# Attention softmax in a fused kernel: epsilon and reciprocal on 128x9 sums ahead of the turn, a copy behind it, and a new written order

## Chip, cores, metric

The kernel runs on one core of a Trainium2 chip. The metric is the device time in microseconds; the time given is the median of several runs, and beside it stands one execution that the hardware profiler recorded.

## What is computed

Causal attention over B = 4, H = 8, S = 576, D = 64 feeds a gated MLP (`moe`), and this feeds a channel mix (`moe2`). The part that the change touches is the division of the softmax:

```python
def _attn_ref(q, k, v, s):
    ...
    scores = np.where(causal, -1000000000.0, scores + np.minimum(bias, 0.0))
    scores = scores - np.max(scores, axis=-1, keepdims=True)
    attn = np.exp(scores)
    attn = attn / (np.sum(attn, axis=-1, keepdims=True) + 1e-09)
    return np.matmul(attn, v).astype(np.float32)
...
def reference(**kwargs):
    ...
    attn_out = _attn_ref(**attn_kwargs)
    ...
    x = _moe_ref(x=x, **moe_kwargs)
    return _moe2_ref(x=x, **moe2_kwargs)
```

All data are 32-bit floats. Products are split into a rounded high part and a remainder, so one product is several matmuls (`ka`/`qa` and `KB`/`QB` for the scores, `wsg0`/`wsg1`, `gh`/`gl` and so on).

## The kernel before

**Attention.** `attn_pair` handles two heads at a time: 16 pairs, numbered 0 to 15, four for each batch. A pair takes nine steps over row tiles of 128: four of the first head (`st<pair>_0_0` to `_0_3`), one with the last 64 rows of both heads (`_2_4`), four of the second head (`_1_0` to `_1_3`). In a step TensorE writes scores into a PSUM bank (`sc`, three banks); VectorE adds the mask, writes the scores to `st` and their row minimum to `mx` (the custom operation, ISA in the order, which is followed by a read of its accumulator into `mx`); ScalarE takes the exponential in place and adds its row sums into one column of `sums0` or `sums1` (128x9, even and odd pairs); TensorE turns the tile (`tp`, and for the last rows `tq`), and ScalarE or VectorE copies it to `pt1` or `pt2` for the product with the values (`pv`, then `xT`). The names in the profile leave the numbers out: `st` is any of the tiles `st5_1_3` and so on.

**End of a pair.** TensorE turns the raw sums (`rt`, 9x128, in PSUM), VectorE adds the epsilon (`rc<-rt`) and takes the reciprocal in place (`rc<-rc`). SyncE stores `rc` in DRAM (`rdram`) and loads it three times, spread over the partitions (`rb`). Later VectorE multiplies `xT` by `rb` (`scale_pending`).

**The rest.** Once a batch has its four pairs, `moe1` runs for it between the pairs of the next batches: `v` and `u` are matmuls whose results go through a gelu on ScalarE and VectorE (steps `v0_2`, `u0_3`: batch 0, tile 2 or 3), `v` is normalised (BN_STATS, BN_AGGR, then `vn`), `sg` mixes along the sequence, and VectorE writes `ga` from it. VectorE also prepares weights in the gaps: `wcs`, `wsg`, `wy`, `syt` are steps of the split of weights, and SyncE stores `wcs` in DRAM (`wscr`). The channel mix with its large products (`k`, `r`) fills the time behind the attention.

**The order.** Each engine runs its instructions in one written order. `ORDER` holds for each engine a list of instruction numbers (numbers in the order in which the code issues them to that engine); `Lines.written` turns the list into the order of the program. An instruction issued with `extra` has no number and stands just ahead of the next numbered one. An engine therefore waits at its next instruction even where a later one could run. Nearly every instruction goes through one helper and so shows as L193 in the profile of before (L194 after the change); the tiles tell them apart.

Of the kernel before, what the change touches and what calls it, by code (L numbers as in the profile page):

```python
# [8 lines left out]
F32 = mybir.dt.float32  # L9
# [3 lines left out]
ALU = mybir.AluOpType  # L13
# [4 lines left out]
P = 128  # L18
# [10 lines left out]
SUM_EPS = 1e-9  # L29
# [51 lines left out]
    ),  # L81
    "vector": (
# [140 lines left out]
def fused_kernel(ctx, tc, kqT, vL, s, w_in, g_ln, w_sgT, b_sg, w_out, mu_k, mu_r, w_k, w_v, w_r, out):  # L223
    nc = Lines(tc.nc)
# [899 lines left out]
```

## Time and profile before

| | before |
|---|---|
| median of 3 runs | 648.51 us (647.1 to 648.82) |
| profiled execution, its own time | 650.21 us |
| profiled execution, span | 648.3 us, mean granted TensorE clock 0.992 |
| TensorE matmul (PE) busy | 619.1 us, 96% of the span |
| TensorE weight load (PEld) busy | 538.1 us, 83% |
| VectorE (DVE) busy | 470.7 us, 73% |
| ScalarE (ACT) busy | 414.7 us, 64% |
| GpSimd (POOL) busy | 244.9 us, 38% |
| chain that ended last | PE 80%, DVE 7%, DMA 6%, ACT 3% |

The span runs from the first to the last instruction of the execution; its own time has 1.9 us more outside it. Busy shares are means over all stages of the kernel; what binds in one stage is read from that stage. A number in brackets in a row of a timeline is the time that the engine sat idle before the row, and behind the arrow stands what ended it. SPq rows are DMAs being issued by SyncE. Successive operations of one engine overlap by a little in the rows, so the distance between two starts is what one costs the queue.

### The profile page before, as it was taken

How to read it: one execution, taken by the hardware profiler on the slowest of the kernel's cores; microseconds unless marked ns; L12 is line 12 of the kernel's file. 1: busy time of each engine (PE TensorE's matmuls, PEld its weight loads, DVE VectorE, ACT ScalarE, POOL GpSimd, SP SyncE). 2: the span in 40 equal slices, each digit the busy share in tenths (PEclk: the TensorE clock that was granted, in tenths of full speed). 3: DMA queues.
4: the chain of work that ended last, by engine and by line, in shares of the span. 5: the costliest groups of instructions: out<-in, count | busy, mean ns of one | idle time of the engine just before them, and what ended most of it. 6: DMA issues, size and time to landing. Idle time of an engine off the chain costs nothing.

```text
span 648.3 us, 11385 instructions
## 1 busy us (share of the span) xinstructions
PE 619.1 (96%) x3768; PEld 538.1 (83%) x3768; DVE 470.7 (73%) x986; ACT 414.7 (64%) x937; POOL 244.9 (38%) x319
## 2 busy tenths in 40 slices
PE   1789999989999999999999999999999999999997
PEld 1667777878778997888897999888888888999997
DVE  6889679995659744569632978478897869696964
ACT  4889889974648834669631864268776778553530
POOL 7466769999629687279371200000000000000000
PEclk9789999999999999999999999999999999999999
DMA  7776574464653643734314974576665794646543
GB/s 216 186 238 198 156 212 110 151 211 114 187 194 94 178 132 81 244 93 135 112 23 146 316 260 125 145 243 199 238 213 196 223 342 151 200 160 206 206 146 122
DMA packets 68522, 115.09 MB, mean 178 GB/s; under 512 B 19744, under 2 KB 32688, under 8 KB 68464
## 3 DMA queue, kind: packets, MB, share of 16 engines
q1 hardware_dynamic: 68464, 114.37, 56.6%
q8 instruction: 30, 0.49, 0.3%
q14 instruction: 28, 0.23, 0.1%
HBM read 75.63 MB, written 29.20 MB: 162 GB/s over the span
## 4 chain that ended last, share of the span: by engine, by line
PE 80%; DVE 7%; DMA 6%; ACT 3%; issue 1%; SPq 1%; POOL 1%; DVEq 0%; ACTq 0%
PE k L193 15%; PE sg L193 8%; PE psa L193 8%; PE r L193 8%; PE o L193 6%; PE sc L193 6%; PE v L193 6%; PE u L193 6%; PE pv L193 6%; PE tp L193 4%; PE psb L193 4%; PE psc L193 2%; DMA wsr<-in_w_sgT_dram 1%; DVE st L193 1%; DMA sraw<-in_w_in_dram 1%
## 5 line engine op out<-in xcount | busy, mean ns | idle before, releaser
L193 PE MATMUL k<-x,wk 128*128 128x512 f32 (+1 forms) x480 | 98.9, 368 | 0.0
L193 PEld LDWEIGHTS k<-x,wk 128*128 128x128 f32 x480 | 83.6, 189 | 14.9
L193 ACT ACTIVATE st<-st,mx 128x384 f32<-128x384 f32 (+4 forms) x128 | 75.1, 588 | 20.2 <-DVE mx L193 18.7
L193 PE MATMUL sc<-ka,qa 128*128 128x512 f32 (+3 forms) x180 | 61.5, 358 | 19.4 <-DMA ka<-ka 13.3
L193 DVE CUSTOM_DVE_ANT_0 st<-sc,mask 128x512 f32<-128x512 f32 (+3 forms) x128 | 62.4, 502 | 13.5 <-PE sc L193 12.5
L193 PE MATMUL sg<-wsg,vn 128*128 128x288 f32 x448 | 63.6, 297 | 0.8 <-DVE ga L193 0.8
L193 PEld LDWEIGHTS sg<-wsg,vn 128*128 128x128 f32 x448 | 60.4, 188 | 1.7 <-DVE ga L193 1.0
L193 PE MATMUL tp<-ident,st 128*128 128x128 f32 x344 | 56.2, 281 | 4.0 <-ACT st L193 3.5
L193 PE MATMUL sc<-KB,QB 128*128 128x512 f32 (+3 forms) x180 | 57.1, 337 | 0.0
L193 PEld LDWEIGHTS sc<-ka,qa 128*128 128x128 f32 x180 | 33.4, 188 | 26.6 <-ACT ka L193 12.5
L193 PEld LDWEIGHTS tp<-ident,st 128*128 128x128 f32 x344 | 42.5, 144 | 10.6 <-ACT st L193 4.2
L193 PE MATMUL pv<-pt,vf 128*64 128x320 f32 (+4 forms) x448 | 51.3, 364 | 0.0
L193 ACT COPY pt<-tp 128x384 f32<-128x384 f32 (+1 forms) x88 | 43.5, 508 | 9.8 <-PE tp L193 9.6
L193 PE MATMUL r<-x,wr 128*128 128x512 f32 (+1 forms) x240 | 49.5, 368 | 0.0
L193 PE MATMUL v<-wv,xs 128*128 128x512 f32 x192 | 48.7, 398 | 0.0
L193 ACT ACTIVATE yx<-yt,mu 128x64 f32<-128x64 f32 (+4 forms) x64 | 30.4, 529 | 27.9 <-DMA yt<-ydram 27.9
L193 PEld LDWEIGHTS r<-x,wr 128*128 128x128 f32 x240 | 41.9, 189 | 7.5
L193 PEld LDWEIGHTS pv<-pt,vf 128*64 128x64 f32 x448 | 29.6, 136 | 20.8 <-issue 3.3
L193 DVE SCALAR_TENSOR_TENSOR yx<-yt,mu,yx 128x64 f32<-128x64 f32 (+4 forms) x64 | 31.1, 514 | 14.6 <-ACT yx L193 14.4
L193 PE MATMUL u<-xs,wc 128*128 128x288 f32 x288 | 41.3, 297 | 0.0
L193 PEld LDWEIGHTS v<-wv,xs 128*128 128x128 f32 x192 | 35.0, 188 | 7.0
L193 PEld LDWEIGHTS u<-xs,wc 128*128 128x128 f32 x288 | 39.2, 188 | 0.5
(184 smaller groups left out, 1420.9 us busy)
## 6 DMA issues: line engine op xcount, KB each, us to landing
wc<-wscr SPq DMA_DIRECT2D x24, 512.0 KB
kq<-in_kqT_dram SPq DMA_DIRECT2D x32, 288.0 KB
kr<-kdram SPq DMA_DIRECT2D x12, 768.0 KB
kdram<-k SPq DMA_DIRECT2D x16, 512.0 KB
yt<-ydram SPq DMA_DIRECT2D x24, 257.0 KB
vf<-in_vL_dram SPq DMA_DIRECT2D x16, 320.0 KB
gt<-gdram SPq DMA_DIRECT2D x12, 384.0 KB
out_dram<-t SPq DMA_DIRECT2D x24, 192.0 KB
```

The source lines that it names most:

```text
L193: r = f(*a, **k)
```

## The change

The epsilon is added and the reciprocal taken on the sums as they lie, 128x9 in SBUF, before TensorE turns them. TensorE then turns the reciprocals, and VectorE copies the turned 9x128 from PSUM to `rc`. The add is an `extra` instruction, so the numbers of all others are kept: the number of the old add is now the reciprocal's, the number of the old reciprocal the copy's. Four of the five lists of `ORDER` are written anew (tensor, vector, scalar, gpsimd; sync is unchanged); of these one line is shown.

```diff
 ORDER = {
...
-        "461 439 443-444 474-475 460 462 465 450 458 466 452 451 476 456 463 467-468 464 469-470 472 471 473 "
+        "461 439 443-444 474-475 460 462 465 450 466 458 452 451 476 456 463 467-468 464 469-470 472 471 473 "
...
+    seps = const.tile([P, 1], F32, tag="seps", name="seps")
...
+    nc.vector.extra(lambda: nc.nc.vector.memset(seps, SUM_EPS))
     nc.gpsimd.memset(mhalf, -0.5)
...
             yield (i + 1) * 200
+        nc.vector.extra(lambda: nc.nc.vector.scalar_tensor_tensor(out=sm, in0=sm, scalar=1.0, in1=seps.broadcast_to([P, 9]), op0=ALU.mult, op1=ALU.add))
+        nc.vector.reciprocal(sm, sm)
         rt = psum1.tile([P, 512], F32, tag="acc", name=f"rt{pr}", bufs=3)
         nc.tensor.transpose(rt[:9, :P], sm, ident)
         rc = at.tile([9, P], F32, tag="rc", name=f"rc{pr}", bufs=1)
-        nc.vector.tensor_scalar_add(rc, rt[:9, :P], SUM_EPS)
-        nc.vector.reciprocal(rc, rc)
+        nc.vector.tensor_copy(rc, rt[:9, :P])
         nc.sync.dma_start(out=rdram[pr], in_=rc)
```

On TensorE `rt` keeps its place among its neighbours, but for pairs 3 and 5, where one matmul or a few change sides. On VectorE three places are shown, before and after; in all of them the last number of a name is a running number of the program and differs between the two.

The first place is VectorE about 41 us into the execution, where pair 1 ends and pair 2 begins. `tq1` is the turned last tile of pair 1, `xT0<-xT0,rb0` the late scaling of pair 0, `wcs0` a weight step. Before:

```order
L193 TENSOR_TENSOR xT0_147<-xT0_147,rb0_309 128x576
L193 ISA st1_1_3_463,mx1_1_3_464<-sc1_1_3_0_465,mask_88 128x512
L193 ISA mx1_1_3_464 128x1
L193 ISA st_f2_555,mx2_0_0_556<-sc2_0_0_0_557,mask_88 128x128
L193 ISA mx2_0_0_556 128x1
L193 COPY pt2_1_366<-tq1_428 128x2x64
L193 TENSOR_TENSOR wcs0_478<-syt4_477,wcs0_478 128x512
L193 ISA st_f2_555,mx2_0_1_562<-sc2_0_1_0_563,mask_88 128x256
```

The same place after the change:

```order
L194 COPY pt2_1_369<-tq1_431 128x2x64
L194 TENSOR_TENSOR xT0_149<-xT0_149,rb0_312 128x576
L194 ISA st1_1_3_466,mx1_1_3_467<-sc1_1_3_0_468,mask_89 128x512
L194 ISA mx1_1_3_467 128x1
L194 TENSOR_TENSOR wcs0_481<-syt4_480,wcs0_481 128x512
L194 ISA st_f2_559,mx2_0_0_560<-sc2_0_0_0_561,mask_89 128x128
L194 ISA mx2_0_0_560 128x1
L194 ISA st_f2_559,mx2_0_1_566<-sc2_0_1_0_567,mask_89 128x256
```

The copy out of `tq1` has moved from behind `st1_1_3` and the first tile of pair 2 to ahead of the scaling of `xT0`, and `wcs0` one step forward.

The second place is VectorE about 98 us into the execution, at the end of pair 5, among the steps of `v` of batch 0. Before:

```order
L193 SCALAR_TENSOR_TENSOR v0_1028<-v0_1028,v0_2_1128 128x512
L193 ISA st5_1_3_1345,mx5_1_3_1346<-sc5_1_3_0_1347,mask_88 128x512
L193 ISA mx5_1_3_1346 128x1
L193 TENSOR_TENSOR wsg1_101<-wsr4_1316,wsg0_100 128x576
L193 SCALAR_TENSOR_TENSOR v0_1028<-v0_1028,v0_2_1128 128x512
L193 COPY pt2_5_1186<-tq5_1281 128x2x64
L193 BN_STATS st6_0_1029<-v0_1028 128x6
L193 ISA st6_0_0_1509,mx6_0_0_1510<-sc6_0_0_0_1511,mask_88 128x128
L193 ISA mx6_0_0_1510 128x1
L193 ISA st6_0_1_1516,mx6_0_1_1517<-sc6_0_1_0_1518,mask_88 128x256
```

And after:

```order
L194 SCALAR_TENSOR_TENSOR v0_1034<-v0_1034,v0_2_1135 128x512
L194 COPY pt2_5_1193<-tq5_1288 128x2x64
L194 ISA st5_1_3_1352,mx5_1_3_1353<-sc5_1_3_0_1354,mask_89 128x512
L194 ISA mx5_1_3_1353 128x1
L194 TENSOR_TENSOR wsg1_102<-wsr4_1323,wsg0_101 128x576
L194 SCALAR_TENSOR_TENSOR v0_1034<-v0_1034,v0_2_1135 128x512
L522 SCALAR_TENSOR_TENSOR sums1_99<-sums1_99,seps_72 128x9
L194 RECIPROCAL sums1_99<-sums1_99 128x9
L194 ISA st6_0_0_1517,mx6_0_0_1518<-sc6_0_0_0_1519,mask_89 128x128
L194 ISA mx6_0_0_1518 128x1
L194 ISA st6_0_1_1524,mx6_0_1_1525<-sc6_0_1_0_1526,mask_89 128x256
```

The copy out of `tq5` has moved ahead of `st5_1_3`; the two new operations on `sums1` stand ahead of `st6_0_0`, and the statistics BN_STATS behind `st6_0_1`.

The third place is VectorE about 128 us into the execution. Pair 6 has ended some time before, and pair 7 is running. Before, the add stood a few rows behind these and the reciprocal behind it:

```order
L193 SCALAR_TENSOR_TENSOR u0_2_1560<-u0_2_1560,u0_2_1_1606 128x288
L193 SCALAR_TENSOR_TENSOR u0_3_1678<-u0_3_1678,u0_3_0_1679 128x288
L193 TENSOR_TENSOR wcs5_1658<-wy5_0_1660,wcs5_1658 128x256
L193 COPY pt2_7_1870<-tp7_0_3_1925 128x4x128
L193 SCALAR_TENSOR_TENSOR u0_3_1678<-u0_3_1678,u0_3_1_1714 128x288
L193 ISA st5_128,mx7_2_4_1931<-sc7_2_4_0_1932,mask_88 128x512
L193 ISA mx7_2_4_1931 128x1
L193 ISA st7_1_0_1980,mx7_1_0_1981<-sc7_1_0_0_1982,mask_88 128x128
L193 ISA mx7_1_0_1981 128x1
L193 TENSOR_SCALAR rc6_1733<-rt6_1731 9x128
```

And after:

```order
L194 SCALAR_TENSOR_TENSOR u0_2_1568<-u0_2_1568,u0_2_1_1614 128x288
L522 SCALAR_TENSOR_TENSOR sums0_98<-sums0_98,seps_72 128x9
L194 RECIPROCAL sums0_98<-sums0_98 128x9
L194 SCALAR_TENSOR_TENSOR u0_3_1686<-u0_3_1686,u0_3_0_1687 128x288
L194 TENSOR_TENSOR wcs5_1666<-wy5_0_1668,wcs5_1666 128x256
L194 COPY pt2_7_1879<-tp7_0_3_1934 128x4x128
L194 SCALAR_TENSOR_TENSOR u0_3_1686<-u0_3_1686,u0_3_1_1722 128x288
L194 ISA st5_130,mx7_2_4_1940<-sc7_2_4_0_1941,mask_89 128x512
L194 ISA mx7_2_4_1940 128x1
L194 ISA st7_1_0_1989,mx7_1_0_1990<-sc7_1_0_0_1991,mask_89 128x128
```

The two operations on `sums0` stand ahead of the steps that lead to `mx7_2_4` and `mx7_1_0`; the copy to `rc6` stands where the add stood, and the place of the old reciprocal, three steps further on, is empty.

## Rows read from the trace of the kernel before

**Rows 1.** Stretches: length, busy us of PE, PEld, DVE, ACT, POOL, clock, DMA
```profile
...
120.00:140.00 20.00, 18.04 (x134) 15.21 (x133) 19.38 (x51) 18.66 (x53) 18.55 (x22) 1.00 0.50 161
...
200.00:300.00 100.00, 100.00 (x689) 85.27 (x687) 66.21 (x181) 65.10 (x170) 70.28 (x95) 1.00 0.48 136
...
```

**Rows 2.** Waits of TensorE: waiter, what ended the wait, total us, times, longest
```profile
...
PE sc L193 <- DVE mx L193: 4.0, 5, 1.4
...
```

**Rows 3.** Tile rc: ns min/median/max, first and last start
```profile
...
L193 DVE TENSOR_SCALAR rc<-rt x16: 268/272/279, 31.4 to 342.6; 9x128 f32<-9x128 f32 x16
L193 DVE RECIPROCAL rc<-rc x16: 929/935/942, 32.6 to 342.9; 9x128 f32<-9x128 f32 x16
...
```

**Rows 4.** Timeline of VectorE, 97 to 105 us: start, us, operation, idle before
```profile
...
97.49 0.18 DVE L193 BATCH_NORM_AGGREGATE mv<-st 128x2 f32<-128x6 f32 x1
97.59 0.66 DVE L193 SCALAR_TENSOR_TENSOR v<-v,v 128x512 f32<-128x512 f32 x1
98.16 0.68 DVE L193 CUSTOM_DVE_ANT_0 st<-sc,mask 128x512 f32<-128x512 f32 x1
...
100.10 0.28 DVE L193 COPY pt<-tq 128x128 f32<-128x128 f32 x1
...
104.82 0.94 DVE L193 RECIPROCAL rc<-rc 9x128 f32<-9x128 f32 x1
```

**Rows 5.** Timeline of VectorE, 25 to 48 us
```profile
...
32.62 0.93 DVE L193 RECIPROCAL rc<-rc 9x128 f32<-9x128 f32 x1
...
41.62 1.17 DVE L193 TENSOR_TENSOR xT<-xT,rb 128x576 f32<-128x576 f32 x1 [1.86 <-ACT xT L193]
...
45.50 1.21 DVE L193 TENSOR_TENSOR wcs<-syt,wcs 128x512 fp32r<-128x512 f32 x1
...
```

**Rows 6.** Timeline of SyncE, which issues the DMAs, 30 to 36 us
```profile
...
33.58 0.30 SPq L193 DMA_DIRECT2D rdram<-rc  x1
...
```

**Rows 7.** Timeline of ScalarE, 26 to 49 us
```profile
...
39.84 0.67 ACT L193 CAST ka_f<-kq 64x576 fp32r<-64x576 f32 x1 [1.85 <-PE sc L193]
...
```

**Rows 8.** Timeline of TensorE, 41 to 44 us
```profile
...
41.83 0.27 PE L193 MATMUL tq<-ident,st 128*128 128x128 f32 x1
...
```

**Rows 9.** Chain of work, 39 to 53 us: start, us, what
```profile
...
47.47 4.42 DMA ka<-ka
...
```

**Rows 10.** Timeline of TensorE, 98 to 100.5 us
```profile
...
98.47 0.27 PE L193 MATMUL tq<-ident,st 128*128 128x128 f32 x1
...
```

**Rows 11.** Timeline of ScalarE, 101 to 105 us
```profile
...
102.16 0.62 ACT L193 ACTIVATE v<-v 128x512 f32<-128x512 f32 x1
...
```

**Rows 12.** Chain of work, 96 to 112 us
```profile
...
101.27 0.30 ACT st L193
...
110.22 0.53 ACT v L193
...
110.77 0.90 DVE v L193
...
```

**Rows 13.** Timeline of VectorE, 128 to 137 us
```profile
...
128.24 0.89 DVE L193 SCALAR_TENSOR_TENSOR u<-u,u 128x288 f32<-128x288 f32 x2
...
132.31 0.93 DVE L193 RECIPROCAL rc<-rc 9x128 f32<-9x128 f32 x1
...
135.06 0.69 DVE L193 CUSTOM_DVE_ANT_0 st<-sc,mask 128x512 f32<-128x512 f32 x1
...
```

**Rows 14.** Timeline of TensorE, 131 to 136 and 142.5 to 146.5 us
```profile
...
131.13 0.39 PE L193 MATMUL sc<-ka,qa 128*128 128x256 f32 x1 [1.15 <-DVE mx L193]
...
134.63 0.39 PE L193 MATMUL sc<-KB,QB 128*128 128x512 f32 x1
...
145.78 0.93 PE L193 MATMUL sg<-wsg,vn 128*128 128x288 f32 x5 [0.78 <-DVE ga L193]
```

**Rows 15.** Timeline of TensorE, 290 to 293 us
```profile
...
292.18 0.27 PE L193 MATMUL rt<-ident,sums 128*9 128x128 f32 x1
...
```

**Rows 16.** Timeline of ScalarE, 288 to 293 us
```profile
...
291.11 0.19 ACT L193 ACTIVATION_READ_ACCUMULATOR st<-st,mx 128x1 f32 x1
...
```

181 rows, old and new, of the table ORDER are left out of this document.

## The prediction

> **What bounds the kernel now.** I read the time by stretches first. From 200 to 300 us TensorE is busy 100.00 of 100.00 while VectorE is busy 66.21; the same full score stands in every later stretch up to the tail. In 120 to 140 TensorE has 18.04 of 20, VectorE 19.38 and ScalarE 18.66 [rows 1]. So the end of the kernel is set by TensorE's work and by the idle time that it collects before some 174 us. A microsecond saved on VectorE counts only where TensorE waits behind VectorE, and a microsecond lost on VectorE counts wherever its queue reaches TensorE before 174. The reader should therefore not multiply the saving of one pair by 16. The waits of TensorE name the candidates: above all 4.0 us in five waits for a row minimum `mx` that VectorE writes [rows 2].
>
> **What is removed, added and kept.** Each of the 16 pairs loses an add (0.272 us) and a reciprocal on 9x128 (0.935) and keeps, in the add's place or the reciprocal's, a copy of the same 9x128 PSUM tile, which I price like the add [rows 3]. It gains two operations on 128x9, which the trace of before does not show. The nearest row is the 128x2 aggregate at 97.49: 0.18 long, and the next operation starts 0.10 after it [rows 4]; the add of 0.272 is the upper bound for the first operation. For the reciprocal the rows give a slope: (0.935 - 0.272) / 128 = 5.2 ns for each column beyond a plain operation, so 9 columns add 0.05 to 0.18, about 0.22 long and 0.14 of the queue; bounds 0.10 (plain) and 0.86 (as 9x128, less the overlap of 0.07). I take 0.25 of queue for the two together, near the aggregate because their width is nearest to its.
>
> The Trainium skill speaks against such an exchange: VectorE: DVE Perf Modes, section "The TRN2 errata", says that SBUF operations pay a fixed cost for each instruction, some 150 cycles by its measured figure, so many small tiles pay it many times. By it each new operation is about 159 / 0.96 = 166 ns, an estimate, so 0.33 for the two where I count 0.25, and the sum would be 0.16 higher over the two pairs that count. The trace bears out the fixed part (0.18 for two columns [rows 4]) but also that 0.08 of it is overlapped.
>
> So VectorE spends 0.272 + 0.935 = 1.21 before and about 0.27 + 0.18 + 0.22 = 0.67 after: 0.54 less in each pair. The count of matmuls, DMAs and ScalarE operations is unchanged; the three loads of `rb` and the store of `rc` stay where they were in SyncE's order. A memset of `seps` at the start I take at nothing: VectorE does it during the first loads.
>
> **Where it can be felt.** Three places before 174.
>
> *27 to 52 us.* Two things of opposite sign. The reciprocal at 32.62 held SyncE: the store of `rc0` is issued at 33.58, right behind it, and the next `kq` load stands behind that store [rows 5, 6]. Without add and reciprocal, and with the copy, `rc0` is ready 0.21 + 0.86 - 0.20 = 0.87 earlier, less about 0.1 for the new pair ahead. ScalarE idles 1.85 before it casts that `kq` at 39.84 [rows 7], so up to 0.77 could come back. Against it, the copy out of `tq1` now stands ahead of the multiply of `xT0`. VectorE would start `xT0` at 41.62 [rows 5], but `tq1` is 41.83 + 0.27 = 42.10 on TensorE [rows 8]; with the copy (0.20) `xT0` starts near 42.34, 0.72 later, and the weight step of 45.50, from whose place the copy is now gone, 0.52 later. SyncE stores that weight ahead of the load of `ka6`, which takes 4.42 us and ends TensorE's wait at 52 [rows 9]. So -0.77 to +0.52. I take 0: the two ends are of one size, and the load may not pass either on in full.
>
> *Pair 5, 97 to 111 us.* The copy out of `tq5` is moved from behind the second `v0_2` step (it ran at 100.10) to ahead of the softmax step `st5_1_3`, which started at 98.16 [rows 4]. But `tq5` ends on TensorE at 98.47 + 0.27 = 98.74 [rows 10]. So `st5_1_3` starts at 98.74 + 0.20 = 98.94, 0.78 late. What is queued behind it: `wsg`, `v0_2`, then the new pair, `st6_0_0`, `st6_0_1`, the statistics (moved back behind `st6_0_1`, so neutral beyond them), `v0_3`. There the delay is 0.78 - 0.20 (the copy is gone from its old place) + 0.25 = 0.83. ScalarE's `v` at 102.16 waits for that `v0_3` step, and the chain of work runs on ScalarE from 101.27 to the end of the `v` of 110.22 without a row of idle time, and VectorE goes on only then, at 110.77 [rows 11, 12]. The reciprocal that falls away in pair 5 stood at 104.82 [rows 4], inside this stretch, where VectorE ends up waiting for ScalarE: it gives nothing. From 110.77 on VectorE is almost without idle time to the wait at 131. So +0.83; bounds 0 (if VectorE is late by that much anyway) and +0.9.
>
> *Pair 6, 128 to 146 us.* The new pair stands behind the `u0_2` step of 128.24, ahead of all that leads to the `mx` for which TensorE waits 1.15 until 131.13 [rows 13, 14]: +0.25 there. The reciprocal that is taken out stood at 132.31, after that wait. Its 0.86 would be a gain if VectorE were then the last; but the step `st7_1_3` at 135.06 [rows 13] needs scores that TensorE finishes at 134.63 + 0.39 = 135.02 [rows 14], and TensorE runs without a gap from 131.13 to there. So TensorE comes 0.25 late, VectorE waits for it, and the freed 0.86 turns into idle time. The chain on to the `ga` at which TensorE waits 0.78 until 145.78 [rows 14] starts from that step. So +0.25; bounds -0.6 (if only VectorE's saving counts) and +0.35.
>
> *The other pairs, 0.* In pair 3 the new operations lie in a wait of VectorE for `rb`, in pairs 0, 4, 7 and 8 they take some tenths that TensorE does not wait for by the rows around. From 174 on the cover is TensorE's own queue. The transpose `rt` now waits for the new pair, and these must be done by then: in the tightest pair, 13, the last exponential's sum is out at 291.11 + 0.19 = 291.30 and `rt` starts at 292.18 [rows 15, 16], 0.88 against 0.25 to 0.33 of new work. If that cover is gone each pair costs what it lacks.
>
> **Sum.** 0 + 0.83 + 0.25 = +1.08. Against the profiled execution's own 650.21 (span 648.3, the rest outside) that is 651.3. That execution is 1.70 above the median of 648.51; none of the two terms that I count lies in a place that I know to be special to it, so I add them to the median: 649.6.
>
> **The rivals.** A measurement of this kernel can tell 0.3%, 1.95 us, from no change: below 646.56 is faster, above 650.46 slower.
>
> *It costs nothing* (0.22): VectorE reaches the moved copies late enough that `tq1` and `tq5` are there, and the rest is hidden: 648.5. For it: in pair 5 only 0.58 separates 98.16 from 98.74. Against it: TensorE was gapless up to `tq5`, so any lateness of VectorE alone costs as much.
>
> *Faster* (0.15): VectorE's saving does reach TensorE. Nine pairs lie before 174; at 0.54 each, and with half of the waits of 4.0 + 0.78 for VectorE closed, 2.4 us come back: 646.1. It decides from 1.95, that is four of nine pairs in full. For it: 19.38 of 20 on VectorE [rows 1], and the new order also shifts other rows whose effect I cannot price. Against it: in pairs 5 and 6 the removed reciprocal stands behind the wait that matters, not ahead of it.
>
> *Slower by TensorE waiting at `rt`* (0.10): in the stretch without gaps each wait is paid in full. Eight pairs, 8 to 15, at 0.3 make 2.4: 650.9; from 0.25 a pair this alone is slower by my bound. Against it: the 0.88 of the tightest pair.
>
> *The 128x9 reciprocal costs what the 9x128 did* (0.08): 0.72 more at pair 5 and at pair 6: 649.6 + 1.4 = 651.0. Then VectorE has lost the advantage altogether. Against it: the slope by columns above.
>
> *My sum* has 0.45; its own range is 648.8 to 650.3, by the bounds of the first place (-0.77, +0.52) and the tops of the other two (+0.07, +0.10).
>
> **The numbers.** 649.6; the range goes from 646.8, the faster rival's near end, to 651.3, past both slower ones, and leaves out about 0.1 on each side. Faster 0.15 (nearly all that rival's); slower 0.27 (the two slower rivals and a fifth of my own case, whose range ends close below 650.46); same 0.58.
>
> **What would show it.** In pair 5: `st5_1_3` behind a copy that waited for `tq5`, ScalarE's `v` 0.8 later against `tq5` than now, and the wait of TensorE near 131 longer by 0.2 to 0.3. VectorE idle ahead of `st7_1_3`. The 128x9 reciprocal 0.2 to 0.25 long; all 16 `rt` without a wait from 174 on, and TensorE full there. I am wrong if the 128x9 reciprocal is above 0.5, if `rt` shows waits, or if TensorE's idle time before 174 falls rather than grows by one microsecond.

## The result

| | time, median | runs | ratio to the kernel before, 95% interval |
|---|---|---|---|
| before, first comparison | 647.91 us | 6 | |
| changed, first comparison | 656.23 us (654.1 to 657.1) | 6 | 1.0124 (1.0103 to 1.0144) |
| before, second comparison | 648.61 us | 23 | |
| changed, second comparison | 654.27 us (652.53 to 656.32) | 6 | 1.0092 (1.0071 to 1.0113) |

The change made the kernel slower by 5.7 to 8.3 us, where 1.1 us was forecast. The page of the changed kernel's profile answers to the table ahead of the prediction:

```profile
span 654.8 us, 11389 instructions
...
PE 626.8 (96%) x3768; PEld 538.7 (82%) x3768; DVE 464.4 (71%) x1003; ACT 415.3 (63%) x937; POOL 242.6 (37%) x319
...
PE 83%; DVE 6%; DMA 4%; ACT 3%; issue 2%; SPq 1%; POOL 0%; DVEq 0%; ACTq 0%
```

VectorE's work fell from 470.7 to 464.4 us, by 6.3 where 16 times the forecast 0.54 would be 8.6. But TensorE, with the same 3768 matmuls, is busy for 626.8 us instead of 619.1. Of these 7.7 us 3.4 lie in the k and r matmuls shown below, and 3.1 in the matmuls that the kernel before ran from 38 to 56 us, where the granted clock of this execution was at its lower level for longer (see the last section). The prediction had no term for TensorE's own work.

The stretches that answer to [rows 1], and one behind them (length, busy us of PE, PEld, DVE, ACT, POOL with the number of instructions, granted clock, DMA share, GB/s):

```profile
120.00:140.00 20.00, 17.44 (x126) 13.98 (x125) 19.04 (x53) 18.84 (x53) 17.88 (x21) 1.00 0.49 151
200.00:300.00 100.00, 99.61 (x676) 83.88 (x675) 63.90 (x186) 64.23 (x168) 68.41 (x95) 1.00 0.46 135
...
420.00:490.00 70.00, 70.00 (x302) 56.23 (x301) 57.68 (x93) 52.33 (x103) 0.00 (x0) 1.00 0.68 224
```

From 420 to 490 us TensorE is full at the full clock, and yet it starts only 302 matmuls. The same stretch in a second trace of the kernel before:

```profile
420.00:490.00 70.00, 70.00 (x310) 57.97 (x309) 58.22 (x90) 51.07 (x101) 0.00 (x0) 1.00 0.68 226
```

310 there. A busy share of 100% in both hides the loss: the rows by tile show it. The k and r matmuls of the changed kernel (count: ns min/median/max, first and last start):

```profile
L194 PE MATMUL k<-x,wk x480: 278/394/397, 408.4 to 513.3; 128*128 128x512 f32 x128, 128*128 128x256 f32 x32
L194 PE MATMUL r<-x,wr x240: 277/394/397, 513.4 to 563.7; 128*128 128x512 f32 x96, 128*128 128x256 f32 x24
```

and of the second trace of before:

```profile
L193 PE MATMUL k<-x,wk x480: 278/389/398, 403.3 to 505.9; 128*128 128x512 f32 x128, 128*128 128x256 f32 x32
L193 PE MATMUL r<-x,wr x240: 278/389/397, 506.1 to 555.2; 128*128 128x512 f32 x96, 128*128 128x256 f32 x24
```

From the first k to the last r it is 563.7 - 408.4 = 155.3 us against 555.2 - 403.3 = 151.9: 3.4 us lost in code that the change does not touch. One matmul of 512 columns starts 233.3 ns after the one ahead of it instead of 226.7 (360 starts in 84.0 and 81.6 us). The psa, psb and psc matmuls that follow take as long as before.

**Where the rest went.** I took the start of the n-th matmul, less that of the n-th in the first trace of before. This distance grows from 98.5 to 144.5 us by 1.69, from 144.5 to 204.0 by 1.16, from 204.0 to 214.1 by 0.45, and in the k and r stage by 3.43; elsewhere behind 98 us by less than 0.1. In the first stretch stand the waits that the prediction spoke of. TensorE of the changed kernel (start, us, operation, idle before):

```profile
121.80 0.50 PE L194 MATMUL sc<-ka,qa 128*128 128x512 f32 x1 [0.59 <-DVE mx L194]
...
132.59 0.39 PE L194 MATMUL sc<-ka,qa 128*128 128x256 f32 x1 [1.36 <-DVE mx L194]
...
147.22 1.06 PE L194 MATMUL sg<-wsg,vn 128*128 128x288 f32 x6 [0.72 <-DVE ga L194]
...
190.77 1.43 PE L194 MATMUL v<-wv,xs 128*128 128x512 f32 x5 [0.44 <-DVE y L194]
```

They answer to [rows 14]: 1.36 for 1.15 ahead of the `mx`, 0.72 for 0.78 ahead of the `ga`. The row at 121.80 has a shorter counterpart in the first trace of before; the one at 190.77 has none:

```profile
120.39 0.50 PE L193 MATMUL sc<-ka,qa 128*128 128x512 f32 x1 [0.25 <-DVE mx L193]
```

### The profile page after: what moved, and what is told of

Read it like the earlier page. It is cut to its first block, busy times and chain, and to the rows that moved or that the text cites. A ratio compares the mean times of both kernels' runs of the same rounds, so it can differ in the third digit from the quotient of the medians.

```text
span 654.8 us, 11389 instructions
## 1 busy us (share of the span) xinstructions
PE 626.8 (96%) x3768; PEld 538.7 (82%) x3768; DVE 464.4 (71%) x1003; ACT 415.3 (63%) x937; POOL 242.6 (37%) x319
## 4 chain that ended last, share of the span: by engine, by line
PE 83%; DVE 6%; DMA 4%; ACT 3%; issue 2%; SPq 1%; POOL 0%; DVEq 0%; ACTq 0%
PE k L194 15%; PE sg L194 8%; PE r L194 8%; PE psa L194 8%; PE sc L194 7%; PE pv L194 7%; PE o L194 6%; PE v L194 6%; PE u L194 6%; PE tp L194 5%; PE psb L194 4%; PE psc L194 2%; DMA vf<-in_vL_dram 2%; DVE st L194 1%; SPq L194 1%
## 5 line engine op out<-in xcount | busy, mean ns | idle before, releaser
L194 PE MATMUL k<-x,wk 128*128 128x512 f32 (+1 forms) x480 | 101.2, 372 | 0.0
L194 PE MATMUL sc<-ka,qa 128*128 128x512 f32 (+4 forms) x180 | 61.7, 360 | 16.6 <-ACT wv L194 11.5
L194 PE MATMUL tp<-ident,st 128*128 128x128 f32 x344 | 58.0, 286 | 2.2 <-ACT st L194 1.9
L194 PEld LDWEIGHTS sc<-ka,qa 128*128 128x128 f32 (+1 forms) x180 | 33.5, 188 | 23.7 <-issue 13.6
```

Source lines behind the costliest of these rows:

```text
L194: r = f(*a, **k)
```

## The experiments

**What else the change moves.** The new tile `seps` has 4 bytes a partition and takes 32. By the addresses in the compiled programs all tiles behind it on its side of SBUF lie 32 bytes higher: x at byte 35872 instead of 35840 (its second place at 19488 instead of 19456), and with it `xs`, `wv`, `wsg`, `u` and `wcs`. The weights `wk` and `wr`, `ka`, `qa`, `vf` and `pt` are laid out from the other end and stay. By the same addresses k and r are, but for 40 turns of tiles early in the attention, the only matmuls whose two operands move against each other; in all others both move or both stay. So my theory was the place in SBUF, and the rival the order and the operations. I tried each alone.

The shift alone:
```diff
 mhalf = const.tile([P, 1], F32, tag="mhalf", name="mhalf")
+const.tile([P, 1], F32, tag="pad", name="pad")
```


> The kernel before with one more tile of 4 bytes a partition in the pool of constants, used by nobody: the operations and the order are those of before, but the x tiles and all else on that side of SBUF lie 32 bytes higher, as in the changed kernel. Theory 'place in SBUF': the matmuls of the k and r stages, 226.7 ns apart before and 233.3 ns in the changed kernel, are again 233.3 ns apart, and that alone adds 3.4 us: about 651.4, and up to 656 if the shift is also behind what the first 210 us lost. Rival 'order and operations': the spacing stays at 226.7 ns and the time at about 648.

The changed kernel without the shift:
```diff
-seps = const.tile([P, 1], F32, tag="seps", name="seps")
-edge.tile([P, 56], F32, tag="edge", name="edge")
+seps = edge.tile([P, 56], F32, tag="edge", name="edge")[:, 55:56]
```


> The changed kernel with epsilon's constant in a tile that was there already, so that no tile moves in SBUF. Theory 'place in SBUF': k and r matmuls 226.7 ns apart, 3.4 us less than the changed kernel, about 652.8; near 649 (the prediction's own sum) if the shift is also behind the losses of 182 to 212 us. Rival 'order and operations': 233.3 ns and about 656.

The new operations in the old order (without the shift), the old operations in the new one. Of VectorE's rows, 31 is pair 0's add, or in the changed code its 128x9 pair, and 32 the operation behind it; the first diff is against the order of before, the second against the new one, and the other pairs are treated alike:
```diff
-... 28 26 29 41 40 42 22 34 44 35 45 31 30 32-33 43 36 ...
+... 28 26 29 41 40 31 42 22 34 44 35 45 30 32-33 43 36 ...
```
```diff
-... 29 41 40 31 42 22 34 44 35 45 30 32 43 33 36 ...
+... 29 41 40 42 22 34 44 35 45 30 31-32 43 33 36 ...
```


> The new operations in the order of before (on VectorE only the pair of new operations is put where the changed kernel has it), and no tile moved in SBUF. If the moved copies of pairs 0, 1 and 5 cost what the prediction said (0.5 and 0.83 us), this is 1 to 1.4 us faster than the same operations in the new order; if the order costs nothing, the two agree within 0.5 us. Against before: the theory of the prediction, that VectorE's saving does not reach TensorE, gives 648 to 648.5; the rival that it does gives 646.

> The old operations in the new order (add and reciprocal on 9x128 both stand where the copy stands), no tile moved in SBUF. If the new order is what costs in the first 210 us: about 650 to 652, with TensorE's new waits near 121, 131 and 190 to 207 us. If the new operations or the place in SBUF do: about 648.

Measured: the shift alone 653.22 us, ratio 1.0053 (1.0028 to 1.0079); the change without it 650.87, 1.0029 (1.0004 to 1.0054); new operations in the old order 651.33, 1.0042 (1.0018 to 1.0066); old operations in the new order 650.86, 1.0031 (1.0004 to 1.0057). The stage of k and r takes 155.4 us with the shift and 151.9 to 152.0 in the three without it. So the theory held, and the rival is refuted for this stage. For the rest, about 0.3%, medians could not part order from operations. The third kernel was no clean test: in it TensorE loses 3.6 us from 98.5 to 144.5 us, with new waits (its rows on TensorE), so it says nothing on the moved copies:

```profile
133.31 0.38 PE L193 MATMUL sc<-ka,qa 128*128 128x256 f32 x1 [1.66 <-DVE mx L193]
...
135.28 1.09 PE L193 MATMUL sg<-wsg,vn 128*128 128x288 f32 x3 [0.32 <-DVE rc L193]
```

**What recurs, and the moved copies.** The changed kernel again, unaltered; and the version without the shift with the copies out of `tq1` (row 49) and `tq5` (143) put back:
```diff
-... 61 49 48 53 56 63-64 ... 127 143 154 147 128 155 ...
+... 61 48 53 56 63 49 64 ... 127 154 147 128 143 155 ...
```


> The changed kernel unaltered, to part what recurs from what one execution had. The runs so far add up to 1.0029 (without the shift) and 3.6 us for the shift, together about 1.0085 of before or 654.8 against 649.3; the first comparison gave 1.0124. If the two stalls that only its first trace shows (0.7 us near 190, where VectorE waits for the reciprocal's broadcast, and half clock for 10 us from 40 on) belong to the change, they are here again and the ratio is 1.011 to 1.014. If they were chance, at least one is gone and the ratio is 1.007 to 1.010.

> The changed kernel without the shift in SBUF, and with the two copies out of tq1 and tq5 put back to their old places on VectorE. Theory (the prediction's terms): the step st5_1_3 starts right behind the step ahead of it, 0.8 us sooner than without the move, and TensorE is 0.5 to 0.8 us less late by 115 us; from 27 to 52 us VectorE loses 0 to 0.7 us less. Together 0.8 to 1.5 us faster than the version without the shift (ratio to before 1.0005 to 1.0017). Rival, the copies are free and the rest of the new order costs: ratio 1.003 as without the shift.

The changed kernel again had 1.0092; its trace has 155.4 us in the k and r stage and no stall at 190 us. The 1.16 us that the first trace lost from 144.5 to 204.0 did not recur (-0.04); seven traces with the operations and order of before have -0.04 to 0.75 there. With the copies put back it was 651.16 us, ratio 1.0036 (1.0015 to 1.0058), no gain by the median; by its trace the stretch of 98.5 to 144.5 us was 1.55 us better than without (-0.28 against +1.27). As the two disagreed I ran both once more, with the kernel before itself, and with the move of `tq5`'s copy alone put into the kernel before:
```diff
-... 127 154 147 128 143 ...
+... 127 143 154 147 128 ...
```


> The kernel before, unaltered, as a second trace of it and as a test of what the comparison can tell. Ratio 1.000 within 0.2%. From 56 us to the end TensorE should keep the distance to the first trace that it has at 56 us within 0.5 us; up to there it may differ by 1 to 2 us, as the other runs of the same operations did (first matmul 10.4 to 13.1 us). If the distance changes by more than 1 us behind 56, single traces can't carry the terms of the sum.

> The kernel before with one row moved: on VectorE the copy out of tq5 stands ahead of the softmax step st5_1_3, as in the changed kernel. Theory (pair 5 of the prediction): st5_1_3 starts 0.8 us later against the step ahead of it, ScalarE's v of 102 us 0.6 us later, and TensorE loses 0.8 us from 98 to 121 us; from the two versions of the changed kernel with and without this move it would be 1.5 us. Rival: the delay goes into a wait that is there anyway, TensorE loses under 0.3 us.

> The changed kernel without the shift and with both copies put back, once more: its trace ended 1.7 us ahead of that of before, its median was 1.0036 of it. If that trace had a lucky start, this one ends later and has its distance at 56 us; if the median of the first comparison was off, the ratio is 1.000 to 1.002 here.

> The changed kernel without the shift in SBUF, once more, on the same chip as the version with the copies put back. Theory: 1.3 us (98 to 146 us) and 0.4 us (204 to 212 us) behind before, ratio 1.0025, and 1 to 1.5 us behind the version with the copies. Rival, the copies are free: the two versions agree within 0.5 us.

Medians and ratios: before itself 649.50, 0.9989 (0.9970 to 1.0008); the move alone 650.52, 1.0010 (0.9990 to 1.0029); copies put back 650.05, 1.0015 (0.9992 to 1.0039); without the shift 650.64, 1.0017 (0.9997 to 1.0037). Medians tell none of these apart. The traces do better: the growth of the distance, in us, in all kernels (the loss in k and r comes after 400 us and leaves these stretches alone; the first trace of before is the zero):

| kernel | 98.5 to 144.5 us | 204.0 to 214.1 us |
|---|---|---|
| before, second trace | -0.72 | 0.03 |
| operations and order of before, tiles moved (five traces) | 0.99, 0.72, 0.75, 0.22, 0.37 | 0.00 to 0.04 |
| before, with the move of tq5's copy | 0.93 | 0.00 |
| changed, no shift, copies put back (two traces) | -0.28, 0.17 | 0.43, 0.46 |
| changed, no shift (two traces) | 1.27, 0.76 | 0.42, 0.47 |
| changed, other places of the tiles (four traces) | 1.69, 1.44, 1.01, 1.42 | 0.43 to 0.49 |
| old operations, new order | 0.76 | 0.46 |
| new operations, old order | 3.61 | 0.46 |

The seven traces with the operations and order of before thus spread from -0.72 to 0.99, with a mean of 0.33, and the 0.93 of the move alone does not stand out from them: in the kernel before its cost is not shown. By the rule set ahead of these runs (no more than 1 us of change behind 56 us) single traces can't carry the terms: from 56.2 to 204.0 us three of these kernels gained 1.1 to 1.7. Means can carry a little more. In the changed kernel the six traces with the copy moved have a mean of 1.26 and the two with it put back -0.06, so the move costs some 1.3 us there. The second pair of traces alone has 0.59 between them, less than the 1 to 1.5 that I expected.

In the rows the move is plain. In all eight traces with it TensorE waits 0.33 or 0.34 us for the `mx` of `st5_1_3`, soon behind `tq5` (here the changed kernel; `tq5` is at 98.28); with the copies put back it does not wait there:

```profile
99.54 0.44 PE L194 MATMUL sc<-ka,qa 128*128 128x384 f32 x1 [0.34 <-DVE mx L194]
```

Of the seven traces with the operations and order of before only one waits at that place, but six wait 0.48 to 1.28 us for a `v` of VectorE just behind it, which none with the move does:

```profile
100.23 2.12 PE L193 MATMUL v<-wv,xq 128*128 128x512 f32 x8 [0.48 <-DVE v L193]
```

So the late copy in part takes the place of a wait that most executions had anyway. VectorE in the kernel before with the move alone:

```profile
93.76 0.65 DVE L193 SCALAR_TENSOR_TENSOR v<-v,v 128x512 f32<-128x512 f32 x1
95.93 0.29 DVE L193 COPY pt<-tq 128x128 f32<-128x128 f32 x1 [1.52 <-PE tq L193]
96.13 0.68 DVE L193 CUSTOM_DVE_ANT_0 st<-sc,mask 128x512 f32<-128x512 f32 x1
```

and in the second trace of the changed kernel with the copies put back:

```profile
95.42 0.65 DVE L194 SCALAR_TENSOR_TENSOR v<-v,v 128x512 f32<-128x512 f32 x1
95.99 0.68 DVE L194 CUSTOM_DVE_ANT_0 st<-sc,mask 128x512 f32<-128x512 f32 x1
...
97.98 0.28 DVE L194 COPY pt<-tq 128x128 f32<-128x128 f32 x1
98.19 0.72 DVE L521 SCALAR_TENSOR_TENSOR sums<-sums,edge 128x9 f32<-128x9 f32 x1
```

In the first the softmax step `st5_1_3` stands behind a copy that waited 1.52 us for the matmul; in the second it starts right behind the step ahead of it. But there the add, some 0.16 us long elsewhere, lasts 0.72. It does not wait for the last sum, which ScalarE has out at 97.86 + 0.19 = 98.05; it ends at 98.91, just behind a step of GpSimd that had begun before it and ends at 98.88:

```profile
97.86 0.19 ACT L194 ACTIVATION_READ_ACCUMULATOR st<-st,mx 128x1 f32 x1
98.14 0.74 POOL L263 TENSOR_TENSOR vn<-v,vn 128x256 fp32r<-128x256 f32 x1
```

This is the rule and not a chance: in nine traces with the new operations 57 of 144 adds last 0.23 to 0.96 us, and each of them ends 0.02 or 0.03 us behind the end of a two-operand step of GpSimd (TENSOR_TENSOR) that ran when the add began; the other 87 take 0.15 to 0.18. The old add, which read PSUM, took 0.27 or 0.28 in all 16 pairs. Part of what the copy gives back is lost again.

**Which place it is.** Two kernels with the operations and order of before: x up by 32 bytes with the pad on the weights' side enlarged, and that pad alone enlarged (`pad` as in the first experiment):
```diff
-edge.tile([P, 56], F32, tag="edge", name="edge")
+edge.tile([P, 64], F32, tag="edge", name="edge")
```


> The kernel before with the x side 32 bytes higher (as in the first experiment) and the other side of SBUF, where the weights wk and wr lie, moved by 32 bytes as well. Theory 'relative place' (the two operands of a matmul must not differ by 32 bytes in their place): k and r matmuls 226.7 ns apart, time as before. Rival 'the moving operand's own place': 233.3 ns and 3.5 us more than before.

> The kernel before with only the weights' side of SBUF moved by 32 bytes; x lies as before. Theory 'relative place': k and r matmuls 233.3 ns apart and 3.5 us more. Rival 'the moving operand's own place': 226.7 ns, time as before.

Measured: 651.49 us, 1.0043 (1.0025 to 1.0060), and 653.03, 1.0070 (1.0048 to 1.0093). The weights moved alone cost as much as x moved alone: 560.7 - 405.3 = 155.4 us from the first k to the last r. So x's own place is not it. But both moved cost 558.7 - 405.9 = 152.8, where the theory wanted 151.9. I had the sign wrong: this side is laid out from the end of SBUF downwards, so a larger pad moves the weights down, away from x. The distance between the operands had changed by 64 bytes, not by 0. The next run tested 64 bytes in another way, in the changed kernel:
```diff
-seps = const.tile([P, 1], F32, tag="seps", name="seps")
+seps = const.tile([P, 16], F32, tag="seps", name="seps")[:, 0:1]
```


> The changed kernel with the new constant's tile made 64 bytes wide a partition, so that all that lies behind it moves by 64 bytes and not by 32. Theory 'relative place by 64': k and r matmuls 226.7 ns apart, the time that of the version without a shift, ratio to before 1.002 to 1.003 (650 to 650.5 against 649). Rival 'any shift': k and r matmuls away from 226.7 ns, about 1.009.

652.53 us, 1.0055 (1.0033 to 1.0077), and 560.2 - 407.3 = 152.9 us in the stage: my theory that only the place within 64 bytes counts fell, and the distance theory was left, with the same 0.9 us for +64 by two routes. It demands that the changed kernel loses nothing once the weights move up with x (first), and I asked for the sign and for 128 bytes in the kernel before (second, third):
```diff
-edge.tile([P, 56], F32, tag="edge", name="edge")
+edge.tile([P, 48], F32, tag="edge", name="edge")
```
```diff
-edge.tile([P, 56], F32, tag="edge", name="edge")
+edge.tile([P, 88], F32, tag="edge", name="edge")
```


> The changed kernel as it is, its new tile included, with the unused pad on the weights' side made 32 bytes smaller, so that wk and wr move up by the same 32 bytes as x. Theory 'distance' (only the distance between the two operands counts, not where either lies): 40 matmuls of the k stage take 9.07 us as before (81.6 us from the 2561st to the 2921st matmul), ratio to before 1.002 to 1.004. Rival 'own place' (an address that is no multiple of 64 costs): 82.4 or 84.0 us in that stretch, ratio 1.006 to 1.010.

> The kernel before with the weights alone moved up by 32 bytes: the distance is changed by -32 instead of +32. If the sign does not count: 84.0 us in that stretch of the k stage, as at +32. If it does: another pace; 81.6 would mean that only one direction costs.

> The kernel before with the weights moved down by 128 bytes: distance +128. If the pattern repeats at 128: 81.6 us in that stretch of the k stage, as at 0. If not: above 81.6, as at +64 (82.4) or +32 (84.0).

| distance of x from wk and wr, against before | kernels | first k to last r, us |
|---|---|---|
| 0 | before; no shift; both up by 32 | 151.9; 152.0; 152.0 |
| +32 | changed; x up by 32; weights down by 32 | 155.3; 155.4; 155.4 |
| -32 | weights up by 32 | 155.5 |
| +64 | x up and weights down by 32; x up by 64 | 152.8; 152.9 |
| +128 | weights down by 128 | 155.1 |

The row for both operands moved up by 32, every tile of the changed kernel in use, is the one that decides:

```profile
L194 PE MATMUL k<-x,wk x480: 278/389/397, 405.1 to 507.8; 128*128 128x512 f32 x128, 128*128 128x256 f32 x32
L194 PE MATMUL r<-x,wr x240: 278/389/398, 507.9 to 557.1; 128*128 128x512 f32 x96, 128*128 128x256 f32 x24
```

The median of 394 ns is 389 again. Its time was 651.78 us, 1.0049 (1.0028 to 1.0071), above what I expected but with an interval that reaches down to the 1.0029 of the version without a shift. The last two kernels were run once, without a ratio (652.59 and 653.08 us). The sign makes next to no difference at 32 bytes, and 128 is no period.

No version of the change beat the kernel before. Without the shift it had 1.0029 and 1.0017, with the copies put back as well 1.0036 and 1.0015; medians can't tell these two apart.

## Why the prediction was wrong

**The step that failed** is a sentence at the end of the part on what is removed, added and kept: "A memset of `seps` at the start I take at nothing". I priced the memset and not the tile. With it went the unsaid premise that a count of matmuls that is unchanged means TensorE's work is unchanged. The tile moves x by 32 bytes against wk and wr, and 720 matmuls in a stage without a gap take 3.4 us more. That is shown from both sides: put into the kernel before, the shift costs it; taken out of the changed one, or matched on the other side, it is gone. A rival "TensorE itself becomes slower" stood nowhere. With the shift priced the sum would have been 649.6 + 3.4 = 653.0, nearer to the 656.23 and 654.27 us measured but still short of both.

**The sum** was +1.08, a ratio of 1.0017. The changed kernel freed of the loss in k and r measured 1.0029, 1.0017 and 1.0049, a mean of 1.0032 or 2.1 us, with intervals that all but the last include the forecast. The traces give the same: six have the new operations and order, seven those of before, and the mean growth of the distance, in us, is

| stretch | forecast | changed | before | difference |
|---|---|---|---|---|
| 12.5 to 56.2 us | 0 | 0.07 | -0.60 | 0.67 |
| 56.2 to 98.5 us | 0 | 0.02 | 0.08 | -0.06 |
| 98.5 to 144.5 us (pairs 5 and 6) | 1.08 | 1.26 | 0.33 | 0.93 |
| 144.5 to 204.0 us | 0 | 0.29 | 0.28 | 0.01 |
| 204.0 to 214.1 us (pair 9) | 0 | 0.45 | 0.02 | 0.43 |

That is 1.98 together; chance leaves 0.1 to 0.35 (one standard error) in each difference, and 0.01 in the last. With the 3.43 of k and r it makes 5.4, of 5.7 us in the second comparison and 8.3 in the first. By its terms:

- *27 to 52 us, 0.* From 12.5 to 56.2 us the distance of the changed operations changed by -1.17 to +0.69 us in six traces with both moves, and by -1.43 to -0.01 in six traces with the operations and order of before. The old operations in the new order, with the moves but without the earlier `rc`, had +1.89. The means lie 0.67 apart, beyond the upper bound of +0.52, with a standard error of 0.34: a loss is likelier than the 0, but it is not settled. (By its own figures `xT0` would start at 42.10 + 0.20 = 42.30, not 42.34; the term of 0 does not hang on that.)
- *Pair 5, +0.83.* The rows are as described. VectorE in the changed kernel, beside [rows 4]:

```profile
97.73 0.66 DVE L194 SCALAR_TENSOR_TENSOR v<-v,v 128x512 f32<-128x512 f32 x1
98.59 0.29 DVE L194 COPY pt<-tq 128x128 f32<-128x128 f32 x1 [0.20 <-PE tq L194]
98.80 0.68 DVE L194 CUSTOM_DVE_ANT_0 st<-sc,mask 128x512 f32<-128x512 f32 x1
...
100.98 0.16 DVE L522 SCALAR_TENSOR_TENSOR sums<-sums,seps 128x9 f32<-128x9 f32 x1
101.17 0.22 DVE L194 RECIPROCAL sums<-sums 128x9 f32<-128x9 f32 x1
101.31 0.23 DVE L194 CUSTOM_DVE_ANT_0 st<-sc,mask 128x128 f32<-128x128 f32 x1
```

  `st5_1_3` starts 0.52 us behind the start of `tq5` (98.28) where it started 0.31 ahead of it: 0.83 late, against 0.78 forecast. ScalarE's `v` starts 103.11 - 98.28 = 4.83 behind `tq5`, before it was 102.16 - 98.47 = 3.69: 1.14 late and not 0.8, as the new pair costs 101.31 - 100.98 = 0.33 of the queue, not 0.25, and the step on `wsg` in between became longer (1.06 us for 0.81; in both traces it ends 0.61 behind a step of GpSimd). So VectorE's lateness is right in place and too small in size. How it reaches TensorE was not foreseen: not first at 131 but a microsecond behind `tq5`, as the wait of 0.34 at 99.54 shown above, and as longer waits for the `mx` at 121.80 (0.25 before, 0.48 to 0.61 in the six changed traces, 1.20 with the move alone). What it costs beside the kernel before can't be parted from pair 6: 0.93 for both, where 1.08 was forecast. That the two agree is in part luck, as the waits are others and the move alone costs 1.3 in the changed kernel.
- *Pair 6, +0.25.* TensorE's wait for `mx` grew by 0.21 in the first trace; over all it is 1.28 to 1.45 in the six changed traces and 1.07 to 1.22 in the seven with the order of before, 0.26 more in the mean, as forecast. The reciprocal that fell away turned into idle time of VectorE, as described (beside [rows 13]):

```profile
136.53 0.69 DVE L194 CUSTOM_DVE_ANT_0 st<-sc,mask 128x512 f32<-128x512 f32 x1 [0.74 <-PE sc L194]
```

- *The other pairs, 0.* Wrong by 0.45 at pair 9. All versions with the new operations or the new order lose 0.42 to 0.49 us from 204.0 to 214.1 us, and those with neither 0.00 to 0.04. In the second trace without a shift TensorE waits there for ScalarE's copy of `xT`; how either cause alone brings that about I did not settle:

```profile
204.33 0.93 PE L194 MATMUL u<-xs,wc 128*128 128x288 f32 x5 [0.23 <-ACT xT L194]
```

- *Prices.* The changed kernel's rows of `rc` and `sums`, beside [rows 3]:

```profile
L194 DVE COPY rc<-rt x16: 268/273/280, 30.2 to 345.7; 9x128 f32<-9x128 f32 x16
...
L522 DVE SCALAR_TENSOR_TENSOR sums<-sums,seps x16: 153/170/936, 26.1 to 342.0; 128x9 f32<-128x9 f32 x16
L194 DVE RECIPROCAL sums<-sums x16: 215/216/218, 26.7 to 342.6; 128x9 f32<-128x9 f32 x16
...
L194 PE MATMUL rt<-ident,sums x16: 270/272/421, 29.7 to 344.9; 128*9 128x128 f32 x16
```

  The copy costs what the add did, the reciprocal 0.216 where 0.22 was forecast, the add in the median 0.17 where 0.18. In the mean the add is 0.32, as 7 of the 16 stand until GpSimd's step has ended (0.24 to 0.94 us); together 2.4 us, about what VectorE's saving falls short of the forecast (8.6 - 6.3). The prediction had no such wait. The rule that the prediction quoted from the Trainium skill (VectorE: DVE Perf Modes, "The TRN2 errata", a fixed cost for each instruction) gave 0.33 for the two in the queue, and this trace agrees where the add does not stand: 0.33 in pair 5, not my 0.25.

**The rivals.** `rt` waits nowhere behind 174 us: in pair 13 the last sum is out at 294.17, the reciprocal done at 294.61, and `rt` starts at 295.26; in pair 8, the tightest now, it is 173.91 and 174.44. The 128x9 reciprocal is not dear. No version with the new operations is faster than before, so VectorE's saving does not bring the 2.4 us of the faster rival; whether some tenths of it reach TensorE in the two traces with the copies put back (-0.06 against 0.33 in the mean) is open. "It costs nothing" is refuted by the means of the traces, most clearly by pair 9.

**What stays open.** The first comparison (1.0124) lies 2.1 us above the second (1.0092), the intervals just overlap. Its trace has the stall at 190 us, and TensorE at half clock from 40 to past 50 us; the second trace has no such stall and a shorter stretch at half clock. Whether the difference between the two is chance I cannot say. Of the 2.9 us that the account leaves of the first comparison, the stall would be 1.16 if the other executions had it too; the rest is unexplained. Why the distance of two operands matters is not shown either: no run altered it for other products; the rows show weight loads (PEld) beside the matmuls, but that the load of the next weights and the stream of x meet in SBUF at some distances is only argued.

## What to carry to other kernels

A new tile is an edit of every tile behind it: compare the addresses of the matmul operands before and after, and if one side moved, move the other by as much or take the new words from a tile that is there. A stage that is 100% busy can still become slower, so compare the count of matmuls in a window, or the first and last start of a tile's rows, not the busy share. Where a change moves a copy within a queue, look for its producer at the new place: the copy that came too early here made TensorE wait 0.33 us in every trace that had it. And where new operations read two tiles in SBUF, look at what GpSimd does at that time, for the price in a quiet stretch (0.16 us) was here half of the mean (0.32).

## What was not expected of the hardware

The pace of 512-column matmuls at the full clock went from 226.7 to 233.3 ns when the distance between the moving and the stationary operand changed by 32 bytes either way: 3.4 us in 720 matmuls, 0.9 us at 64 bytes and 3.2 at 128. The loss is in the 576 matmuls of 512 columns; the steps of the 144 of 256 columns are 2 to 3 ns shorter than before. The psa, psb and psc matmuls keep their pace (173.3 ns apart, each 334 ns long, in both), but they are no counterexample: both of their operands lie on the side that moved, so their distance is the old one. Whether 384 columns would suffer was not tried. The Trainium skill (SBUF — State Buffer, "SBUF: two separate sides") says that on the engines' side only the port shared by GpSimd and VectorE causes contention and that TensorE waits for nobody; read as covering TensorE's own two operands too, that rule would have the shift cost nothing. The measurement differs and decides: with both operands moved alike, 152.0 us, with one moved, 155.4.

VectorE's add on two tiles in SBUF stood until a step of GpSimd that was already running had ended, in 57 of 144 cases, for up to 0.8 us; the add on the turned sums in PSUM never did. What the two engines share there no run parts.

The granted clock early in the kernel differs from one execution to the next. In the first trace of the changed kernel it is at its lower level, 1.2 GHz, from 40 us to past 50, after TensorE had worked 0.77 of 2 us; in its second trace from 42 to 49, and in the first trace of before for less than 4 us about 46:

```profile
38.00:40.00 2.00, 0.77 (x5) 0.53 (x5) 0.10 (x2) 2.00 (x6) 1.92 (x3) 1.00 0.40 48
40.00:42.00 2.00, 1.56 (x6) 1.19 (x7) 2.00 (x5) 1.48 (x5) 1.94 (x3) 0.51 0.97 341
...
48.00:50.00 2.00, 2.00 (x13) 1.39 (x11) 0.58 (x3) 2.00 (x4) 1.92 (x3) 0.50 0.49 187
50.00:52.00 2.00, 2.00 (x16) 1.55 (x12) 1.50 (x5) 1.12 (x6) 1.93 (x4) 0.93 0.35 85
```

Two traces of one kernel differ by 0.6 to 2.6 us in what they gain from 12.5 to 56.2 us (four kernels with two traces each). How much of that is the clock was not measured.
